# Column results of five experts turned by VectorE in 32x32 squares and scattered as quarter rows

## The chip, the cores and the metric

The kernel runs on one core of one Trainium2 chip. The metric is the device time of one execution in microseconds. The kernel before takes 846.96 us, the median of three runs (845.41 to 847.40). Five engines are named here as the profile names them: PE (TensorE, with PEld for its weight loads), DVE (VectorE), ACT (ScalarE), POOL (GpSimd) and SP (the queue that issues most DMAs).

## The reference, cut to what matters

Over 2048 tokens of 512 features the program returns `x + A(xn) + B(xn)`, where `xn` is the layer norm of `x`, A is a linear attention block and B a mixture of eight experts. Only B is touched here:

```python
logits = xf @ w_gate                       # 8 experts, each token takes its two best
gates = softmax(topk_val)
for e in range(E):                         # xf: (2048, 512), w1: (512, 1792), w2: (1792, 512)
    w = (gates * (topk_idx == e)).sum(-1, keepdims=True)
    out = out + w * (silu(xf @ w1[e]) @ w2[e])
```

## The kernel before, in words

The first quarter of the program (up to about 200 us) does the layer norm, the attention block and the routing. The rest goes through the experts in the order of how many tokens they have, numbered r = 0 to 7. Expert r has room for CAP[r] tokens: 576, 552, 544, 528, 520 for r = 0 to 4 and 512 for the others. The 1792 hidden features are taken in seven pairs j = 0 to 6 of 256; `g = 7 r + j` counts the pairs through.

**One pair.** `pair_fast` computes 256 hidden features in seven products (px, pz, py, L1129) with fp32r matmuls. Each operand is a high and a low part, which ACT and DVE make from a loaded weight (`split_hi` L126, `split_lo` L129). Between the products it calls `fill(k)`, which issues the waiting matmuls of the second layer (`mm2`) of the pair before, and `jobs(k)`, which issues the work that `plan` has put into slot k (0 to 6) of this pair. So the order on every engine's queue is written out by hand, and all engines take their instructions in that order.

**The second layer.** `mm2` adds up `h @ w2` in PSUM over all 14 hidden tiles. For the first 256 tokens of an expert with more than 512 places the result has the tokens on the partitions (L1058, "by token"). For the other 264 to 320 tokens the result is turned: the 512 output features stand on the partitions in four accumulators and the tokens in the columns (L1061, "by column"). The experts r = 5 to 7 (`single`) are by token altogether.

**Getting the results out.** By token: `put` multiplies by the token's gate on the way out of PSUM (DVE L1033 or ACT L1031) into a tile `yo`, and POOL adds `yo` to the rows of `out` in DRAM with an indirect accumulating DMA (L1035), after a small memset that it uses as a spacer (L1034). By column: ACT copies each accumulator into a tile `yt` (L1071); two pairs later `y_out` lets PE turn four 128x128 blocks of `yt` into a PSUM tile `yp` (L1093, a tile of the tag `mm`, which px, pz and py use too), and `put` on ACT, the memset and the scatter follow. There are three `y_out` for each of the five experts; `plan` puts two ahead of the first product of pair j = 2 of the next expert and one ahead of that of j = 3. Each scatter waits for the scatters of the expert before (`scat`).

**Weights.** SP loads w1 and w2 of each pair into one of three stage buffers as soon as one of them is free (`fetch_w`, L824 and L828). The w1 of a pair is used first by four DVE sums (`w1_sums`, L862 to L866), then by splits; w2 by splits only (`w2_hi`, `w2_lo`).

**The next expert's tokens.** POOL gathers them by indirect DMA (L921) in pair j = 3, two experts ahead; SP writes them to a DRAM scratch and reads them back (L975, L983); DVE turns them in 32x32 squares (`x_turn`, L992).

Of the kernel before, what the change touches and what calls it, by code (L numbers as in the profile page):

```python
# [72 lines left out]
def linear_attn_plus_moe(  # L73
# [132 lines left out]
    def constants_b():  # L206
        def iota(t, pattern, base=0, cm=0):
            G.iota(t, pattern=pattern, base=base, channel_multiplier=cm,
                   allow_small_or_imprecise_dtypes=True)

        G.memset(eps6, 1e-6)
        G.memset(ones, 1.0)
        G.affine_select(out=tri_b, in_=ones_b, pattern=[[1, P]], compare_op=ALU.is_ge,
                        fill=0.0, base=-1, channel_multiplier=-1)
        G.affine_select(out=bmask, in_=ones.rearrange("p (a b) -> p a b", a=8),
                        pattern=[[-DH, 8], [0, DH]], compare_op=ALU.is_ge,
                        fill=0.0, base=0, channel_multiplier=1)
# [162 lines left out]
    gate = rt.tile([P, OV0], F32, name="gate")  # L380
    eid_i = rt.tile([P, E], I32, name="eid_i")
    trip_i = rt.tile([P, 1], I32, name="trip_i")
    gidx = rt.tile([P, NB], I32, name="gidx")
    sidx = rt.tile([P, NB], I32, name="sidx")

# [206 lines left out]
    def table_end():  # L592
# [5 lines left out]
        V.scalar_tensor_tensor(sidx, t1, -1.0, em, op0=ALU.add, op1=ALU.add)  # L598
        Q.dma_start(gi_d, gidx[:, OV0:])
        Q.dma_start(si_d, sidx[:, OV0:])  # L600

    def side_jobs():
        yield from routing()
# [229 lines left out]
    def plain_w():  # L833
        if plain[0] > NPLAIN:
            return
        m, (r, j) = items[plain[0]]
        plain[0] += 1
        w = (W1, W2)[m][r, j] = hilo(sm, f"w{m}_{r}_{j}", (KC, 2)[m])
        split(w[0], w[1], wst.pop((m, r, j)))
        fetch_w()  # L840

    def w2_hi(r, j, i):
        if i == 0:
            W2[r, j] = hilo(sm, f"w2_{r}_{j}", 2)
        split_hi(W2[r, j][0][:, i, :], wst[1, r, j][:, i, :])

    def w2_lo(r, j, i):
        split_lo(W2[r, j][0][:, i, :], W2[r, j][1][:, i, :], wst[1, r, j][:, i, :])
        if i == 1:
            wst.pop((1, r, j))  # L850
            fetch_w()
# [175 lines left out]
    def put(r, i, src, w, eng):  # L1027
        b = r * RB + i
        yo = ta(f"yo{r}_{i}")
        if eng is A:  # L1030
            A.activation(yo[:w], src[:w], AF.Copy, scale=gate[:w, b:b + 1])  # L1031
        else:
            V.tensor_scalar(yo[:w], src[:w], gate[:w, b:b + 1], None, op0=ALU.mult)  # L1033
        G.memset(spacer, 0.0)  # L1034
        st = G.indirect_dma_start(out=out, out_offset=IOA(ap=sidx[:w, b:b + 1], axis=0),  # L1035
                                  in_=yo[:w], in_offset=None, compute_op=ALU.add).ins
        for s_ in scat[r]:
            tc.declare_no_dep(st, s_, reason="an expert's places hold different rows")
        for s_ in scat.get(r - 1, ()):
# [7 lines left out]
    def mm2(r, n, d):  # L1047
# [17 lines left out]
        if tok:  # L1065
            put(r, by_token(r)[d], ya[r, d], P, (V, A)[d % 2])
            return
        q = d - nt
        if q % 2 == 0:
            yt[r, q // 2] = raw(um(f"yt{r}_{q}"))[:, :2 * (N - nt * P)].rearrange("p (k c) -> p k c", k=2)  # L1070
        A.activation(yt[r, q // 2][:, q % 2, :], ya[r, d], AF.Copy)  # L1071

    def nacc(r):
        return 4 if single(r) else 2 + KC
# [21 lines left out]
    def pair_plain(r, j, fill, jobs, held):  # L1096
        n = half(r)
# [268 lines left out]
    def plan(g):  # L1366
# [44 lines left out]
                on(k, f, r + 1, name)  # L1411
        if r > 0 and j == 0:
            on(0, x_lo, r, "T4")
        if r > 0 and not single(r - 1):
# [134 lines left out]
```

## Time and profile before

| | value |
|---|---|
| median of three runs | 846.96 us (845.41 to 847.40) |
| the profiled execution | 845.64 us, of which the span of its instructions is 844.0 us |
| PE busy | 834.8 us (99%) |
| DVE, ACT, POOL busy | 80%, 64%, 21% of the span |
| granted clock of PE | 1.0 of full speed over the span |

The span runs from the first to the last instruction that the profile shows; 1.64 us of the profiled execution lie outside it. Busy shares are means over stages of different kinds, and a matmul's end is modelled, so PE's own rows say how often a matmul starts better than how long one lasts. An idle time is put down to what ended it.

### The profile page before, as it was taken

To read this page: it belongs to the slowest core of one execution; us is meant where nothing else is said; L and a number is where in the kernel's file an instruction comes from. 1 tells how busy PE (TensorE), PEld (TensorE's weight loads), DVE (VectorE), ACT (ScalarE), POOL (GpSimd) and SP (SyncE) were. 2 spreads that over 40 slices of the span, in tenths; PEclk is the share of its full clock that TensorE was granted. 3 is DMA by queue.
4 is the path that set the end of the run, shared out by engine and by line. 5 is a ranking of instruction groups with operands and counts; after the bars stand their busy time and mean duration, and the time that the engine had idled before them with its cause. 6 is when DMAs were issued, how large, how long until landed. Compare 5 with 4: busy or idle time off the path is not lost.

```text
span 844.0 us, 15824 instructions
## 1 busy us (share of the span) xinstructions
PE 834.8 (99%) x5454; PEld 764.2 (91%) x5454; DVE 676.0 (80%) x1495; ACT 539.0 (64%) x1127; POOL 178.6 (21%) x200
## 2 busy tenths in 40 slices
PE   8999999999999999999999999999999999999997
PEld 7899878788999999999999999999989999999986
DVE  7888888988878877888788778779888887987741
ACT  5566454348566766766777677667767766776740
POOL 2432224374410122014102300320130030020011
PEclk9999999999999999999999999999999999999999
DMA  5542036454755565566556744755665573349416
GB/s 178 165 159 75 26 107 216 132 178 162 219 165 140 155 138 162 134 158 161 154 136 166 178 122 138 166 153 147 160 167 145 146 189 100 100 118 265 131 15 163
DMA packets 94997, 124.23 MB, mean 147 GB/s; under 512 B 12354, under 2 KB 57794, under 8 KB 94882
## 3 DMA queue, kind: packets, MB, share of 16 engines
q1 hardware_dynamic: 86210, 103.18, 41.1%
q0 software_dynamic: 7840, 18.57, 11.1%
q10 hardware_dynamic: 864, 1.44, 0.5%
q8 instruction: 44, 0.72, 0.3%
q14 instruction: 39, 0.32, 0.1%
HBM read 93.56 MB, written 30.91 MB: 147 GB/s over the span
## 4 chain that ended last, share of the span: by engine, by line
PE 88%; DVE 7%; DMA 1%; ACT 1%; issue 1%; POOL 1%; SPq 0%; POOLq 0%; DVEq 0%
PE y L1058 25%; PE px L1129 19%; PE y L1061 13%; PE pz L1129 9%; PE k L325 5%; PE py L1129 5%; PE gacc L370 4%; PE op L1238 3%; PE qp L1187 2%; PE yp L1093 1%; DMA xg<-xn_d,gidx 1%; PE xtp L287 1%; DMA x<-in_A_x_dram 1%; PE hp L1108 1%; DVE den L1215 1%
## 5 line engine op out<-in xcount | busy, mean ns | idle before, releaser
L1035 POOL DMA_INDIRECT out_dram<-yo,sidx x37 | 61.2, 1654 | 486.4 <-DVE yo L1033 408.4
L129 DVE TENSOR_TENSOR h<-hs,h 128x512 fp32r<-128x512 f32 (+5 forms) x112 | 78.5, 701 | 6.9 <-ACT h L126 6.6
L126 ACT ACTIVATE h<-hs 128x512 fp32r<-128x512 f32 (+5 forms) x112 | 72.5, 647 | 2.9
L1137 ACT ACTIVATE hs<-px 128x256 f32<-128x256 f32 (+5 forms) x54 | 21.1, 391 | 57.8 <-PE px L1129 57.8
L1152 ACT ACTIVATE hs<-hs 128x256 f32<-128x256 f32 (+5 forms) x54 | 23.1, 427 | 46.9 <-DVE hs L1151 46.9
L1156 DVE TENSOR_TENSOR hs<-px,hs 128x256 f32<-128x256 f32 (+5 forms) x54 | 23.4, 434 | 33.9 <-PE px L1129 33.9
L1151 DVE TENSOR_TENSOR hs<-pz,hs 128x256 f32<-128x256 f32 (+5 forms) x54 | 23.3, 432 | 30.8 <-PE pz L1129 30.8
L370 PE MATMUL gacc<-pkhl,xnhl 128*128 128x512 f32 x192 | 47.8, 398 | 0.0
L921 POOL DMA_INDIRECT xg<-xn_d,gidx x37 | 42.3, 1143 | 25.8 <-issue 11.2
L1162 DVE TENSOR_TENSOR hs<-py,hs 128x256 f32<-128x256 f32 (+5 forms) x54 | 23.4, 433 | 24.2 <-PE py L1129 24.2
L370 PEld LDWEIGHTS gacc<-pkhl,xnhl 128*128 128x128 f32 x192 | 34.9, 188 | 6.9 <-DVE pkhl L129 0.2
L1157 ACT ACTIVATE hs<-hs 128x256 f32<-128x256 f32 (+5 forms) x54 | 22.9, 424 | 20.7 <-DVE hs L1156 19.4
L1058 PE MATMUL y<-w_0h,h 128*128 128x512 f32 x88 | 33.8, 403 | 0.0
L1058 PE MATMUL y<-w_1h,h 128*128 128x512 f32 x88 | 32.6, 398 | 0.0
L1058 PE MATMUL y<-w_2h,h 128*128 128x512 f32 x88 | 32.5, 396 | 0.0
L1058 PE MATMUL y<-w_3h,h 128*128 128x512 f32 x88 | 32.5, 395 | 0.0
L1147 ACT ACTIVATE hs<-px 128x256 f32<-128x256 f32 (+5 forms) x54 | 21.2, 392 | 17.6 <-PE px L1129 16.7
L1058 PE MATMUL y<-w_4h,h 128*128 128x512 f32 x88 | 32.0, 394 | 0.0
L1058 PE MATMUL y<-w_6h,h 128*128 128x512 f32 x88 | 31.7, 394 | 0.0
L1058 PE MATMUL y<-w_5h,h 128*128 128x512 f32 x88 | 31.6, 393 | 0.0
L1196 ACT ACTIVATE e_q<-qp 128x512 f32<-128x512 f32 x16 | 9.6, 600 | 33.0 <-PE qp L1187 18.3
L354 POOL TENSOR_TENSOR zacc<-zacc,pk 128x512 f32<-128x512 f32 x14 | 18.1, 1296 | 50.2 <-DVE L L347 50.2
(517 smaller groups left out, 3112.5 us busy)
## 6 DMA issues: line engine op xcount, KB each, us to landing
wst<-in_B_w_dram SPq DMA_DIRECT2D x63, 512.0 KB, 3.7
wst<-in_B_w_dram SPq DMA_DIRECT2D x196, 128.0 KB, 2.5
xs_d<-xg SPq DMA_DIRECT2D x117, 64.0 KB, 1.8
xq<-xs_d SPq DMA_DIRECT2D x28, 256.0 KB, 4.0
x<-in_A_x_dram SPq DMA_DIRECT2D x27, 256.0 KB, 3.3
xn_d<-xn SPq DMA_DIRECT2D x16, 256.0 KB, 2.5
out_dram<-x SPq DMA_DIRECT2D x11, 256.0 KB, 2.2
out_dram<-zt SPq DMA_DIRECT2D x5, 256.0 KB, 4.2
```

The lines of the kernel that those rows point to most:

```text
L126: A.activation(hi, src, AF.Copy)
L129: V.tensor_tensor(lo, src, raw(hi), op=ALU.subtract)
L325: T.matmul(o, xT(t, a, kc), w[b][:, kc, :], start=(j == 0), stop=(j == 11))
L370: T.matmul(gacc[d], xnhl[:, a, d * P:(d + 1) * P], pkhl[:, b, :], start=(t == 0 and i == 0), stop=(t == NT - 1 and i == 2))
L921: G.indirect_dma_start(out=t, out_offset=None, in_=xn_d, in_offset=IOA(ap=gidx[:, b:b + 1], axis=0))
L1035: st = G.indirect_dma_start(out=out, out_offset=IOA(ap=sidx[:w, b:b + 1], axis=0), in_=yo[:w], in_offset=None, compute_op=ALU.add).ins
L1058: T.matmul(ya[r, d], h[a][:, d * P:(d + 1) * P], w[b][:, n % 2, :], start=(first and i == 0), stop=(last and i == 2))
L1061: T.matmul(ya[r, d], w[a][:, n % 2, (d - nt) * P:(d - nt + 1) * P], h[b][:, nt * P:], start=(first and i == 0), stop=(last and i == 2))
L1129: T.matmul(ps_, w[a][:, o + kc, :], x[b][:, kc, :], start=(start and kc == 0 and i == 0), stop=(kc == 1 and i == 2), skip_group_check=True)
L1156: V.tensor_tensor(c22, px, c22, op=ALU.add)
L1162: V.tensor_tensor(c11, pz_, c11, op=ALU.add)
L1238: T.matmul(op, pqT[t][:, a, kc * P:(kc + 1) * P], M_v[kc // 2][b][:, kc % 2, :], start=(kc == 0 and i == 0), stop=(kc == KC - 1 and i == 2))
```

## The change

PE no longer turns the column results. `yt` is padded to a multiple of 32 tokens; POOL multiplies it by the gates (`y_gate`), which lie along the columns now and come as a row broadcast to all partitions through DRAM (`gate_out`, `gate_in`); DVE turns it in 32x32 squares into a tile `yu` (`y_turn`); POOL scatters it in groups of 32 tokens, where each partition holds a quarter of a token's row (`y_put`). For this the columns of w2 are written in another order when they are split (`columns`, `squares`), and results by token are put back in order on their way out of PSUM (`in_order`). `places` makes the row numbers of the quarter rows, once. `YMOVES` says in which pair, slot and for which expert each step is issued. The diff without the parts that only declare tiles or set constants (two DRAM scratch tensors, five POOL memsets, three views):

```diff
+YMOVES = {0: ((6, "i", -1),),
+          1: ((0, "g", -1, 0), (1, "g", -1, 1)),
+          2: ((0, "o", 0),),
+          3: ((3, "t", -1, 0, 0), (5, "t", -1, 0, 1)),
+          4: ((0, "p", -1, 0), (1, "t", -1, 1, 0), (2, "t", -1, 1, 1), (3, "t", -1, 2, 0), (4, "t", -1, 2, 1),
+              (5, "p", -1, 1), (6, "p", -1, 2))}
...
+    def columns(r, ap):
+        return ap if single(r) else ap.rearrange("p (a k i) -> p k a i", a=4, i=BLK)
+
+    def squares(r, ap):
+        return ap if single(r) else ap.rearrange("p (k a i) -> p k a i", a=4, i=BLK)
+
+    def in_order(r, ap):
+        return ap if single(r) else ap.rearrange("p (k a i) -> p a k i", a=4, i=BLK)
...
-        split_hi(W2[r, j][0][:, i, :], wst[1, r, j][:, i, :])
+        split_hi(squares(r, W2[r, j][0][:, i, :]), columns(r, wst[1, r, j][:, i, :]))
...
-        split_lo(W2[r, j][0][:, i, :], W2[r, j][1][:, i, :], wst[1, r, j][:, i, :])
+        hi, lo = (squares(r, W2[r, j][h][:, i, :]) for h in range(2))
+        split_lo(hi, lo, columns(r, wst[1, r, j][:, i, :]))
...
+        frm = in_order(r, src[:w])
+        to = yo[:w] if single(r) else yo[:w].rearrange("p (a k i) -> p a k i", a=4, i=BLK)
         if eng is A:
-            A.activation(yo[:w], src[:w], AF.Copy, scale=gate[:w, b:b + 1])
+            A.activation(to, frm, AF.Copy, scale=gate[:w, b:b + 1])
         else:
-            V.tensor_scalar(yo[:w], src[:w], gate[:w, b:b + 1], None, op0=ALU.mult)
+            V.tensor_scalar(to, frm, gate[:w, b:b + 1], None, op0=ALU.mult)
+        scatter(r, out, sidx[:w, b:b + 1], yo[:w])
+
+    def scatter(r, rows, idx, src):
         G.memset(spacer, 0.0)
-        st = G.indirect_dma_start(out=out, out_offset=IOA(ap=sidx[:w, b:b + 1], axis=0),
-                                  in_=yo[:w], in_offset=None, compute_op=ALU.add).ins
+        st = G.indirect_dma_start(out=rows, out_offset=IOA(ap=idx, axis=0), in_=src, in_offset=None,
+                                  compute_op=ALU.add).ins
...
+            if n < n_:
+                G.memset(yt[r, q // 2][:, :, n:], 0.0)
+        A.activation(yt[r, q // 2][:, q % 2, :n], ya[r, d], AF.Copy)
...
-    def y_out(r, k, tag="mm"):
+    def places(k):
+        if k == 0:
+            s_at = ta("s_at", BLK)
+            V.transpose(s_at, s_of)
+            Q.dma_start(sx_d, s_at)
+            ta_in.append(ta("s_in", P))
+            s_in = ta_in[0].rearrange("p (c j) -> p c j", j=BLK)
+            for a in range(4):
+                Q.dma_start(s_in[a * BLK:(a + 1) * BLK], sx_d.rearrange("(c b) j -> b c j", b=BLK))
+        else:
+            s_in = ta_in.pop().rearrange("p (c j) -> p c j", j=BLK)
+            s_up = ta("s_up", P).rearrange("p (c b) -> p c b", b=BLK)
+            V.transpose(s_up, s_in)
+            V.tensor_scalar(sidx4, s_up, 4.0, part, op0=ALU.mult, op1=ALU.add)
+
+    def gate_out(r):
+        if not single(r):
+            b = r * RB + 2
+            Q.dma_start(gate_d[r].rearrange("(b p) -> p b", p=P), gate[:, b:b + 3])
+
+    def gate_in(r):
+        if not single(r):
+            gb[r] = ta(f"gb{r}", 3 * P)
+            Q.dma_start(gb[r], gate_d[r:r + 1].broadcast_to([P, 3 * P]))
+
+    def y_gate(r, q):
+        if not single(r):
+            y = yt[r, q]
+            G.tensor_tensor(y, y, gb[r][:, :y.shape[2]].unsqueeze(1).broadcast_to(list(y.shape)), op=ALU.mult)
+
+    def y_turn(r, k, q):
         if single(r):
             return
         i, o, w = by_column(r)[k]
-        p = psm(tag, f"yp{r}_{k}")
-        for d in range(KC):
-            T.transpose(p[:w, d * P:(d + 1) * P], yt[r, d // 2][:, d % 2, o:o + w], ident)
-        put(r, i, p, w, A)
+        c = -(-w // BLK)
+        if q == 0:
+            yu[r, k] = ta(f"yu{r}_{k}")[:, :c * P].rearrange("p (c f) -> p c f", f=P)
+        V.transpose(yu[r, k][:, :, q * 2 * BLK:(q + 1) * 2 * BLK].rearrange("p c (k i) -> p c k i", i=BLK),
+                    yt[r, q][:, :, o:o + c * BLK].rearrange("p k (c j) -> p c k j", j=BLK))
+
+    def y_put(r, k):
+        if not single(r):
+            y = yu.pop((r, k))
+            for c in range(y.shape[1]):
+                scatter(r, out.rearrange("s (a f) -> (s a) f", a=4), sidx4[:, c, 3 * r + k:3 * r + k + 1], y[:, c])
...
-            for k in {2: (0, 1), 3: (2,)}.get(j, ()):
-                front.insert(k % 2, lambda k=k: y_out(r - 1, k))
+        for k, f, e, *a in YMOVES.get(j, ()):
+            if 0 <= r + e < E:
+                on(k, (gate_out, gate_in, y_gate, y_turn, y_put)["oigtp".index(f)], r + e, *a)
+        if g in (2, 4):
+            on(6, places, g // 2 - 1)
```

In `YMOVES` the key is the pair j, and in each entry stand the slot, the step (i `gate_in`, g `y_gate`, o `gate_out`, t `y_turn`, p `y_put`), the expert counted from the one in work, and the step's own arguments.

## Rows read from the trace of the kernel before

**Rows 1.** The page of the profiled execution: the first line is the span, the second the busy time of each engine with its share of the span and its instructions.

```profile
span 844.0 us, 15824 instructions
PE 834.8 (99%) x5454; PEld 764.2 (91%) x5454; DVE 676.0 (80%) x1495; ACT 539.0 (64%) x1127; POOL 178.6 (21%) x200
```

**Rows 2.** The chain of waits that ended last, summed by line (shares of the span).

```profile
by line: PE y L1058 25.3%; PE px L1129 18.8%; PE y L1061 13.2%; PE pz L1129 9.4%; PE k L325 4.9%; PE py L1129 4.7%; PE gacc L370 3.6%; PE op L1238 2.9%; PE qp L1187 2.0%; issue 0.8%; PE yp L1093 0.8%; DMA xg<-xn_d,gidx 0.7%; PE xtp L287 0.7
```

**Rows 3.** The instructions that write or read the tile `yp`, whole span. Behind the count: shortest, median and longest duration in ns, first and last start in us, shapes.

```profile
L1093 PEld LDWEIGHTS yp<-ident,yt x60: 84/139/146, 300.1 to 625.5; 128*128 128x128 f32 x40, 128*64 128x64 f32 x4, 128*40 128x40 f32 x4, 128*32 128x32 f32 x4
L1093 PE MATMUL yp<-ident,yt x60: 270/272/277, 300.3 to 625.6; 128*128 128x128 f32 x40, 128*64 128x128 f32 x4, 128*40 128x128 f32 x4, 128*32 128x128 f32 x4
L1031 ACT ACTIVATE yo<-yp,gate x15: 677/688/695, 301.0 to 625.9; 128x512 f32<-128x512 f32 x10, 64x512 f32<-64x512 f32 x1, 40x512 f32<-40x512 f32 x1, 32x512 f32<-32x512 f32 x1
```

**Rows 4.** The timeline of PE, first around the two `y_out` of expert 0 (start us, length us, then the instruction), then three matmuls of 512 columns elsewhere.

```profile
300.28 0.60 PE L1093 MATMUL yp<-ident,yt 128*128 128x128 f32 x4
300.64 0.48 PE L1058 MATMUL y<-w_0h,h 128*128 128x512 f32 x1
...
301.42 0.60 PE L1093 MATMUL yp<-ident,yt 128*128 128x128 f32 x4
301.77 0.48 PE L1058 MATMUL y<-w_0h,h 128*128 128x512 f32 x1
...
302.55 0.42 PE L1129 MATMUL px<-xB,wa_2h 128*128 128x276 f32 x2
...
319.10 0.39 PE L1058 MATMUL y<-w_2h,h 128*128 128x512 f32 x1
319.33 0.40 PE L1058 MATMUL y<-w_2l,h 128*128 128x512 f32 x1
319.56 0.63 PE L1058 MATMUL y<-w_2h,h 128*128 128x512 f32 x2
```

**Rows 5.** Busy time by stretch. A stretch goes from one pair's first copy out of px (L1137) to the next pair's. The columns are the stretch, its length, busy us and instructions of PE, PEld, DVE, ACT and POOL, the granted clock, the share of the DMA engines and GB/s. The first six stretches belong to expert 5 (pairs j = 0 to 5; the three `y_out` of expert 4 fall into the second and third), the last three to expert 6 (j = 0 to 2, without any `y_out`).

```profile
594.94:606.02 11.08, 11.08 (x84) 10.55 (x83) 9.61 (x20) 8.22 (x20) 0.13 (x1) 1.00 0.53 155
606.02:617.05 11.03, 11.03 (x73) 9.89 (x72) 9.05 (x24) 8.00 (x18) 5.21 (x6) 1.00 0.80 183
617.05:628.05 11.00, 11.00 (x72) 9.80 (x71) 9.10 (x22) 7.33 (x17) 2.84 (x5) 1.00 0.66 143
628.05:638.59 10.54, 10.54 (x68) 9.51 (x67) 8.29 (x18) 6.75 (x15) 4.62 (x6) 1.00 0.73 203
638.59:649.12 10.53, 10.53 (x68) 9.51 (x67) 7.42 (x16) 7.65 (x17) 0.00 (x0) 1.00 0.37 102
649.12:659.66 10.54, 10.54 (x68) 9.53 (x67) 9.57 (x20) 7.65 (x18) 0.00 (x0) 1.00 0.57 149
670.19:681.12 10.93, 10.93 (x71) 9.91 (x70) 9.45 (x20) 7.93 (x18) 1.22 (x1) 1.00 0.47 145
681.12:691.26 10.14, 10.14 (x65) 9.12 (x64) 8.98 (x24) 6.75 (x17) 5.47 (x8) 1.00 0.99 226
691.26:701.79 10.53, 10.53 (x68) 9.52 (x67) 8.87 (x22) 6.75 (x15) 0.00 (x0) 1.00 0.48 135
```

**Rows 6.** Groups of DVE instructions by line, tile and shape: count, busy us and mean ns of one, then idle time before them.

```profile
L992 DVE STREAM_TRANSPOSE xr<-xq 128x256 f32<-128x256 f32 x56 | 21.4, 420 | 0.0
L129 DVE TENSOR_TENSOR pkhl<-pk,pkhl 128x512 fp32r<-128x512 f32 x16 | 14.2, 889 | 0.8 <-ACT pkhl L126 0.7
L129 DVE TENSOR_TENSOR w_6l<-wst,w_6h 128x512 fp32r<-128x512 f32 x16 | 10.9, 683 | 0.0
L129 DVE TENSOR_TENSOR wa_3l<-wst,wa_3h 128x512 fp32r<-128x512 f32 x8 | 5.5, 681 | 0.0
```

**Rows 7.** The same of POOL's instructions.

```profile
L1035 POOL DMA_INDIRECT out_dram<-yo,sidx x37 | 61.2, 1654 | 486.4 <-DVE yo L1033 408.4 <-ACT yo L1031 73.7 <-issue 1.3
L1034 POOL MEMSET spacer<- 1x1 f32 x37 | 19.3, 521 | 7.2 <-issue 7.2
L354 POOL TENSOR_TENSOR zacc<-zacc,pk 128x512 f32<-128x512 f32 x14 | 18.1, 1296 | 50.2 <-DVE L L347 50.2
```

**Rows 8.** The timeline of POOL at two scatters that follow each other.

```profile
291.28 1.64 POOL L1035 DMA_INDIRECT out_dram<-yo,sidx  x1 [55.29 <-DVE yo L1033]
292.35 0.61 POOL L1034 MEMSET spacer<- 1x1 f32 x1
293.22 1.57 POOL L1035 DMA_INDIRECT out_dram<-yo,sidx  x1 [0.26 <-issue]
```

**Rows 9.** DMA queues of the page (packets, MB, share of 16 engines' span): q1 carries what SP issues, q0 POOL's gathers and scatters.

```profile
q1 hardware_dynamic: 86210, 103.18, 41.1%
q0 software_dynamic: 7840, 18.57, 11.1%
```

**Rows 10.** The timeline of SP in pairs j = 4 and 5 of expert 5: loads of w1 (four issues) and w2, and eight writes of 64 KB in rows of 512 bytes. The last row is the issues of the four-part loads of w1, with the median us from issue to landing at its end.

```profile
637.87 1.87 SPq L824 DMA_DIRECT2D wst<-in_B_w_dram  x4
644.32 0.39 SPq L828 DMA_DIRECT2D wst<-in_B_w_dram  x1
...
650.64 3.75 SPq L975 DMA_DIRECT2D xs_d<-xg  x8
...
wst<-in_B_w_dram SPq DMA_DIRECT2D x196, 128.0 KB, 2.5
```

**Rows 11.** The timeline of DVE in the same pairs: the first use of the w1 that was issued at 637.87.

```profile
645.88 0.42 DVE L862 TENSOR_TENSOR wr<-wst 128x256 f32<-128x256 f32 x1
```

More of the change, by code (lines that the diff above doesn't have):

```diff
@@ L35 @@
 CAP = (576, 552, 544, 528, 520, 512, 512, 512)
+NCOL = sum(c > 4 * 128 for c in CAP)
 UW = 2 * CAP[0]
@@ L99, in linear_attn_plus_moe @@
     xs_d = tc.dram_tile((E * RB * P, D), F32, name="xs_d")
+    gate_d = tc.dram_tile((E, 3 * P), F32, name="gate_d")
+    sx_d = tc.dram_tile((P, BLK), F32, name="sx_d")
     def ta(name, w=D, dt=F32):
@@ L231, in constants_b @@
             G.memset(i_cap[:, r:r + 1], float(CAP[r]))
+        G.memset(gate, 0.0)
+        for a in range(4):
+            G.memset(part[a * BLK:(a + 1) * BLK], float(a))
         G.affine_select(out=lower, in_=ones[:, :E * E].rearrange("p (a b) -> p a b", a=E),
@@ L382, in linear_attn_plus_moe @@
     trip_i = rt.tile([P, 1], I32, name="trip_i")
+    s_of = i_e8.rearrange("p t e -> p (t e)")[:, :BLK]
+    part = rt.tile([P, 1], F32, name="part")
+    sidx4 = L.rearrange("p t e -> p (t e)").bitcast(I32).rearrange("p (c b) -> p c b", b=BLK)
     gidx = rt.tile([P, NB], I32, name="gidx")
@@ L600, in table_end @@
         Q.dma_start(si_d, sidx[:, OV0:])
+        t3, e3 = (a[:, :NCOL * RB].rearrange("p (r i) -> p r i", i=RB)[:, :, 2:] for a in (t1, em))
+        V.scalar_tensor_tensor(s_of[:, :3 * NCOL].rearrange("p (r i) -> p r i", i=3), t3, -1.0, e3,
+                               op0=ALU.add, op1=ALU.add)
     def side_jobs():
@@ L838, in plain_w @@
         w = (W1, W2)[m][r, j] = hilo(sm, f"w{m}_{r}_{j}", (KC, 2)[m])
-        split(w[0], w[1], wst.pop((m, r, j)))
-        fetch_w()
+        st = wst.pop((m, r, j))
+        if m:
+            for i in range(2):
+                split(squares(r, w[0][:, i, :]), squares(r, w[1][:, i, :]), columns(r, st[:, i, :]))
+        else:
+            split(w[0], w[1], st)
+        fetch_w()
+    def columns(r, ap):
[4 more added lines that the diff above has]
+        return ap if single(r) else ap.rearrange("p (k a i) -> p a k i", a=4, i=BLK)
     def w2_hi(r, j, i):
@@ L1067, in mm2 @@
             return
-        q = d - nt
+        q, n = d - nt, N - nt * P
+        n_ = -(-n // BLK) * BLK
         if q % 2 == 0:
-            yt[r, q // 2] = raw(um(f"yt{r}_{q}"))[:, :2 * (N - nt * P)].rearrange("p (k c) -> p k c", k=2)
-        A.activation(yt[r, q // 2][:, q % 2, :], ya[r, d], AF.Copy)
+            yt[r, q // 2] = raw(um(f"yt{r}_{q}"))[:, :2 * n_].rearrange("p (k c) -> p k c", k=2)
+            if n < n_:
+                G.memset(yt[r, q // 2][:, :, n:], 0.0)
+        A.activation(yt[r, q // 2][:, q % 2, :n], ya[r, d], AF.Copy)
     def nacc(r):
@@ L1085, in pieces @@
         return [lambda c=c, d=d: mm2(r, c, d) for c, d in order]
-    def y_out(r, k, tag="mm"):
+    gb, yu = {}, {}
+    ta_in = []
+    def places(k):
[5 more added lines that the diff above has]
+            s_in = ta_in[0].rearrange("p (c j) -> p c j", j=BLK)
+            for a in range(4):
+                Q.dma_start(s_in[a * BLK:(a + 1) * BLK], sx_d.rearrange("(c b) j -> b c j", b=BLK))
+        else:
+            s_in = ta_in.pop().rearrange("p (c j) -> p c j", j=BLK)
[15 more added lines that the diff above has]
+    def y_turn(r, k, q):
         if single(r):
@@ L1413, in plan @@
             on(0, x_lo, r, "T4")
-        if r > 0 and not single(r - 1):
-            for k in {2: (0, 1), 3: (2,)}.get(j, ()):
-                front.insert(k % 2, lambda k=k: y_out(r - 1, k))
+        for k, f, e, *a in YMOVES.get(j, ()):
[3 more added lines that the diff above has]
+            on(6, places, g // 2 - 1)
         if j == 3 and r in (E // 2, E - 1):
```

## The prediction

> **What bounds the kernel now.** I read the page first: PE is busy 99% of a span of 844.0 us, DVE 80%, ACT 64% and POOL 21% [rows 1]. A busy PE need not be the limit, since ends of matmuls are modelled, so the chain of waits came next: 71% of it is PE's second layer and products (L1058, L1061, L1129), most of the rest PE's earlier matmuls, and the turning of the column results (L1093) has 0.8% [rows 2]; 0.8% of 844 is 6.75 us. The decisive view is the busy time by stretch. In expert 6, where nothing is turned, a pair takes 10.53 us, and so does a pair of expert 5 with DVE 7.42 us busy and one with DVE 9.57 us busy (10.54 us) [rows 5]. The pair does not get longer when DVE has 2 us more to do, so PE's stream of matmuls sets its length, and DVE can fill 91% of a pair without showing. What is taken off PE in these stages should come off the time, until another engine or a load is late.
>
> **What the change removes.** Sixty PE transposes in fifteen `y_out`, and fifteen evictions on ACT of 688 ns [rows 3]. A transpose's own 272 ns is no price, because matmuls overlap; I count from start to start. From 300.28 to 302.55 PE starts two `y_out` of four transposes and six matmuls of 512 columns: 2.27 us. Such a matmul otherwise starts every 0.23 us (319.10, 319.33, 319.56), six take 1.38, and (2.27 - 1.38) / 2 = 0.44 us is left for one `y_out` [rows 4]. A second reading: the two stretches of expert 5 that hold the three `y_out` of expert 4 last 11.03 + 11.00 = 22.03 us, the same two of expert 6 10.14 + 10.53 = 20.67; the difference of 1.36 us is 0.45 for each [rows 5]. All have a moving side of 128 columns, the short last blocks too [rows 3], so fifteen cost 6.6 us (0.44) to 6.8 us (0.45). All of it is on PE's chain. I take 6.6. ACT's 10.3 us hide nothing, ACT has a third of each stretch free [rows 5]. The buffer of the tag `mm` that `yp` took comes free for px and pz; since PE shows no idle time in those stretches, I count nothing for it.
>
> **What it adds.**
>
> *DVE.* Per expert four transposes of 256 columns and two of 64 or 128. `x_turn` makes the same kind with the same 32-wide runs: 420 ns for 256 columns [rows 6]. With at most 0.28 us for a short one (estimate, between half of it and a little more) that is 4 x 0.42 + 2 x 0.28 = 2.2 us per expert, 0.84 in pair j = 3 and 1.4 in j = 4. There DVE is busy 8.29 of 10.54 and 7.42 of 10.53 us [rows 5], and gets 9.1 and 8.8, less than the 9.57 that costs nothing in j = 5. Price: 0. Without that cover it would be at most 11 us for the five experts.
>
> *The order of w2's columns.* Splits on ACT and DVE read 32-wide runs instead of 512 in one piece; by-token evictions likewise. The number of elements stays. A split whose source is strided (128-wide runs) takes 681 ns, one in a piece 683 [rows 6]. So I take 0, and can't see a gain. No row has a split with 32-wide runs; were it twice as long, DVE would get 2 x 0.68 us more in a pair j = 5 with 0.97 us free [rows 5], and the loss were 0.4 us in each of the ten fullest pairs, 4 us: the upper bound. One w2 split of pair 0 becomes two halves, 2 x 0.68 us on DVE, once: 0 (within 0.3).
>
> *POOL.* Ten `y_gate` of 528 to 640 columns. The sum into `zacc` takes 1296 ns for 512 [rows 7], so 1.3 to 1.6 us each, 15 us in all. Scatters: groups of 32 tokens make 4 + 4 + (2, 2, 1, 1, 1) for the five experts, 47 in the place of 15. One follows another after 1.94 us, memset and all [rows 8]; a train of ten takes 19.4 us, from j = 4 to the end of j = 5, where POOL is idle (0.00 busy) [rows 5]. In order behind the train stand only the next expert's pads and token scatters, more than a pair later, and the gathers of j = 3 come ahead of it. Price: 0. The fronts of the train wait for DVE's `y_turn`, and only their own train waits behind them. `y_gate` waits for the gates' DMA; behind it on POOL are the gathers, two pairs later.
>
> *The port between POOL and DVE.* A split beside POOL's sums into `zacc` (`pkhl`) takes 889 ns on average, 683 elsewhere [rows 6], 0.2 us more. Two `y_gate` in j = 1 put 0.4 us on DVE's 9.05 of 11.03 us [rows 5]: hidden. At worst a DVE instruction waits out the whole of a 1.3 us `y_gate`; two of these are 2.6 us against 1.98 free, 0.6 us per expert, 3 us in all.
>
> The Trainium skill, GPSIMD Engine Reference, section 1 (Specifications), says that POOL's way to SBUF is shared with VectorE and contended by DVE instructions with two SBUF inputs, which the splits are. By that rule every split beside `y_gate` loses time and the sum goes towards the 3 us; the 889 ns above agree that there is such a loss, and show it as 0.2 us.
>
> *SP.* `gate_out` and `gate_in` are ten small DMAs, each issued pairs ahead of its use. `places` stops SP once, in pair 2 of expert 0: its read-back waits for its write to land, and the next weight load stands behind. A w1 load issued from 637.87 to 639.74 lands 2.5 us later, about 642.2, and is first used at 645.88 [rows 10, 11]: 3.7 us to spare. Price 0, at most 2 us once.
>
> **Sum.** -6.6 us on PE, all else hidden: 845.64 - 6.6 = 839.0 us for the profiled execution. The median of the runs shown is 1.3 us above that execution, 846.96, so the forecast is **840.4 us**.
>
> **Rivals.**
>
> *The gain is eaten by DVE.* The upper bounds above come together: 4 us from split order, 3 from the port, and the time is 846.96 - 6.6 + 7 = 847.4, no change; half of it gives 843.9. For it: DVE is the second busiest engine, and 9.57 of 10.54 us leaves little. Against it: the stretch with 9.57 us is no longer than that with 7.42, and none of the new transposes falls in j = 5 or 6.
>
> *The quarter rows clog the DMA engines and weights come late (slower).* 1440 whole-row packets (ten blocks of 128 tokens and 160 tokens in the short ones) become 47 x 128 = 6016 of 512 bytes, 1200 per expert within the train's 19.4 us. A packet of q0 takes 0.111 x 16 x 844 / 7840 = 0.19 us on average [rows 9]. If an accumulating packet costs this whatever its size, a train needs 1200 x 0.19 / 16 = 14.3 us of all sixteen engines. With the other traffic at 0.57, the share of j = 5 [rows 5], 8.3 us are free; loads come 6.0 us late, 3.7 are spare, and PE loses 2.3 us per expert, 11.5 in all: 846.96 - 6.6 + 11.5 = 851.9 us. It turns the sign when the loss passes 1.3 us per expert, at (8.3 + 3.7 + 1.3) x 16 / 1200 = 0.18 us per packet. Against it: packets of q1, 1.2 KB on average, take 0.411 x 16 x 844 / 86210 = 0.064 us [rows 9], and SP sends eight writes of 128 rows of 512 bytes in 3.75 us [rows 10], which is 0.06 us per packet if the engines keep up. Twice that, for a read and a write, is 0.12 and stays below the point. Also, a stretch with the engines at 0.99 of their time kept its 10.14 us [rows 5].
>
> The Trainium skill, DMA: Bandwidth & Descriptors, section Bandwidth, speaks for this rival: transfers under 64 KB are dominated by their descriptors, and here whole-row scatters of 256 KB are cut to 64 KB. By that rule the packets would not get cheaper as they get shorter and the time is the 851.9 above; q1's packets speak against it, and no row has a short accumulating one.
>
> **How the numbers follow.** Forecast 0.68 (own range 839.5 to 842); part or all of the gain eaten by DVE 0.19, of which 0.07 still gains over 0.3%; DMA late 0.13, mostly slower. A measurement of this kernel tells 0.3%, 2.5 us, from no change. So faster 0.74, same 0.13, slower 0.13. The range goes from 838.6 (6.8 us of gain, and 1.55 us by which the lowest of the three runs lies under their median) to 846.0, which takes in most of the second case; the third is left out.
>
> **What would show it.** Right: no L1093; the second and third stretch of experts 1 to 5 shorter by 0.89 and 0.46 us and all other stretches as before; transposes of 0.42 us into `yu`; w2 splits at 0.68; trains of scatters at 1.9 us and POOL at about 0.9 in j = 4 and 5; PE without idle time. Wrong in its first step: L1093 gone and the stretches as long as before. DVE's case: PE waits for DVE at px or pz in j = 1 or 5, splits of w2 above 0.8 us. DMA's case: packets of q0 near 0.19 us still, and DVE or ACT waiting for `wst` in j = 5 and 6. The forecast is wrong if the median is above 844.4.

## The result, and the profile after

The changed kernel takes **852.43 us** (median of 20 runs, 847.61 to 858.84) against 846.95 us (20 runs, 845.31 to 850.21): 1.0071 times as long, with an interval of 1.0058 to 1.0085. The forecast was 840.4 us, the range ended at 846.0, and the change is slower by 5.5 us. The profiled execution is a long one of 856.27 us, with a span of 854.5.

These lines of its page stand beside [rows 1, 2, 7, 9]: span, busy times, queues, the chain by line, and the group of the quarter-row scatters.

```profile
span 854.5 us, 15872 instructions
PE 833.5 (98%) x5394; PEld 761.6 (89%) x5394; DVE 692.5 (81%) x1530; ACT 529.9 (62%) x1113; POOL 251.4 (29%) x285
...
q1 hardware_dynamic: 89650, 104.25, 43.6%
q0 software_dynamic: 12896, 18.71, 13.2%
...
PE y L1096 23%; PE px L1210 17%; PE y L1099 11%; PE pz L1210 9%; PE k L337 5%; PE py L1210 4%; PE gacc L382 4%; DMA wst<-in_B_w_dram 3%; PE op L1319 3%; PE qp L1268 2%; DVE h L138 1%; DVE w_1l L138 1%; DMA xg<-xn_d,gidx 1%; PE xtp L299 1%; DMA x<-in_A_x_dram 1%
...
L1073 POOL DMA_INDIRECT out_dram<-yu,L x47 | 78.7, 1675 | 99.3 <-DVE yu L1168 88.4
```

PE's 60 transposes are gone (5454 to 5394 matmuls) and yet the span is 10.5 us longer, with 21 us instead of 9 in which PE does nothing. The weight load `wst` has 3% of the chain, some 25 us; it is not among the lines of [rows 2].

Busy time by stretch, cut and with columns as in [rows 5]. The first four are pairs j = 1 to 4 of expert 2, the fifth is j = 4 of expert 4, the last two are j = 1 and 2 of expert 5.

```profile
373.37:384.17 10.80, 10.80 (x76) 10.15 (x75) 9.06 (x21) 6.96 (x16) 8.33 (x7) 1.00 0.82 206
384.17:395.63 11.46, 11.46 (x79) 10.71 (x78) 7.09 (x19) 7.06 (x15) 3.40 (x5) 1.00 0.98 170
395.63:413.67 18.04, 13.41 (x80) 12.79 (x80) 12.23 (x28) 7.16 (x15) 1.59 (x2) 0.81 0.36 83
413.67:424.86 11.19, 11.19 (x80) 10.68 (x79) 9.30 (x23) 7.96 (x18) 9.58 (x13) 1.00 0.71 129
569.55:584.60 15.05, 12.26 (x79) 11.72 (x80) 11.70 (x27) 7.91 (x18) 11.00 (x14) 0.89 0.55 106
617.05:627.18 10.13, 10.13 (x65) 9.11 (x64) 8.77 (x20) 6.75 (x17) 7.33 (x6) 1.00 0.89 213
627.18:637.71 10.53, 10.53 (x68) 9.51 (x67) 8.53 (x22) 6.53 (x15) 3.27 (x4) 1.00 0.81 203
```

The last two are the stretches that held `y_out`: 20.66 us where they were 11.03 + 11.00 [rows 5], so the gain on PE is there. But one pair took 18.04 us and another 15.05 where the same pairs take 11.18 and 10.69 when nothing is late (in gate_rows below). In the first, PE stands idle for 18.04 - 13.41 = 4.63 us, and its busy time is 13.41 - 11.18 = 2.23 us more than the same 80 matmuls take there, at a granted clock of 0.81.

What the pair of 18.04 us waits for, from three views: SP's timeline (start, length), the chain in order of time, and busy time in slices of 2 us (columns as in [rows 5]).

```profile
384.94 2.10 SPq L842 DMA_DIRECT2D wst<-in_B_w_dram  x4
387.08 0.44 SPq L1149 DMA_DIRECT2D gate_d<-gate  x1
...
391.23 0.39 SPq L846 DMA_DIRECT2D wst<-in_B_w_dram  x1
```

```profile
386.75 11.25 DMA wst<-in_B_w_dram
...
398.13 0.44 DVE wr L895
...
399.70 0.62 DVE h L138
...
400.36 0.85 PE y L1099 x2
```

```profile
394.00:396.00 2.00, 1.73 (x11) 1.37 (x9) 0.00 (x0) 0.56 (x2) 0.00 (x0) 1.00 0.35 34
396.00:398.00 2.00, 0.00 (x0) 0.00 (x0) 0.00 (x0) 0.03 (x1) 0.00 (x0) 0.98 0.54 58
398.00:400.00 2.00, 0.00 (x0) 0.00 (x0) 1.84 (x5) 0.63 (x1) 0.00 (x0) 0.50 0.56 115
400.00:402.00 2.00, 1.64 (x7) 1.65 (x8) 2.00 (x5) 0.00 (x0) 0.00 (x0) 0.50 0.14 49
402.00:404.00 2.00, 2.00 (x10) 2.00 (x10) 1.27 (x3) 0.92 (x2) 0.00 (x0) 0.50 0.38 109
404.00:406.00 2.00, 2.00 (x16) 2.00 (x14) 0.92 (x3) 0.82 (x2) 0.00 (x0) 0.82 0.55 152
```

The last part of a w1 load, issued at 386.75, lands after 11.25 us instead of 2.5 [rows 10]. DVE waits for it with its first sum (L895), the split of `h` for the second layer stands behind that sum in DVE's order, and PE waits for `h`. While PE is idle its clock falls to 0.50, which is the level of 1.2 GHz; it starts again at 400.36, gets 10 matmuls of the usual 16 or so into 2 us, and has its full clock back between 404 and 406. So the late load costs 4.63 us of idle time and 2.23 us of slow matmuls.

Right behind the w1 load SP issues `gate_out` (L1149): three columns of `gate`, 384 values of four bytes each, written next to each other in DRAM. In the same stretch of time the DMA engines look like this (slice, granted clock, DMA share, GB/s; a packet counts with its whole time in the slice in which it begins, so a share can pass 1):

```profile
388.00:390.00 2.00, 1.00 0.98 273
390.00:392.00 2.00, 1.00 0.95 237
392.00:394.00 2.00, 1.00 2.06 35
```

The packets that begin between 392 and 394 take over twice all sixteen engines' time in sum, while 35 GB/s get through, and 34 in the next 2 us. The scatters of quarter rows are not there yet, so they are not the cause. What is there is a gather (POOL's timeline):

```profile
381.73 1.29 POOL L954 DMA_INDIRECT xg<-xn_d,gidx  x1
...
387.67 1.14 POOL L954 DMA_INDIRECT xg<-xn_d,gidx  x1 [0.72 <-issue]
...
412.08 1.82 POOL L1073 DMA_INDIRECT out_dram<-yu,L  x1 [23.18 <-DVE yu L1168]
414.21 1.80 POOL L1073 DMA_INDIRECT out_dram<-yu,L  x1 [0.26 <-issue]
```

The gathers are put into pair j = 3 by the plan, but they run in j = 1 and 2 of this expert: in POOL's queue nothing stands ahead of them any more that waits for late data, as `y_out`'s scatters did. In the kernel before, the first of the same gathers comes some 15 us later, behind such a scatter (POOL's timeline there):

```profile
394.94 1.66 POOL L1035 DMA_INDIRECT out_dram<-yo,sidx  x1 [8.43 <-ACT yo L1031]
396.91 1.04 POOL L921 DMA_INDIRECT xg<-xn_d,gidx  x1 [0.30 <-DVE h L129]
```

So there were three theories. **G**: `gate_out`'s short neighbouring writes hold up the DMA engines. **T**: the early gathers collide with the w1 loads. **P**: the port between POOL and DVE, where `y_gate` stretches DVE's instructions; it would explain the smaller losses of 0.3 to 1.6 us in the pairs j = 2 of experts 1 to 4. The prediction's DMA rival, that quarter rows clog the engines, is a fourth, and every run that keeps the quarter rows and is fast speaks against it. In the texts put down before the runs G is theory A (A1 and A2 are two readings of it), T is rival B, the quarter rows are rival C, and P is theory D.

### The profile page after: what moved, and what is told of

It reads as the page before. It is cut to its first block, busy times and chain, and to the rows that moved or that the text cites. A ratio compares the mean times of both kernels' runs of the same rounds, so it can differ in the third digit from the quotient of the medians.

```text
span 854.5 us, 15872 instructions
## 1 busy us (share of the span) xinstructions
PE 833.5 (98%) x5394; PEld 761.6 (89%) x5394; DVE 692.5 (81%) x1530; ACT 529.9 (62%) x1113; POOL 251.4 (29%) x285
## 3 DMA queue, kind: packets, MB, share of 16 engines
q0 software_dynamic: 12896, 18.71, 13.2%
## 4 chain that ended last, share of the span: by engine, by line
PE 78%; DVE 11%; DMA 5%; ACT 1%; issue 1%; SPq 1%; POOL 1%; DVEq 0%; POOLq 0%
PE y L1096 23%; PE px L1210 17%; PE y L1099 11%; PE pz L1210 9%; PE k L337 5%; PE py L1210 4%; PE gacc L382 4%; DMA wst<-in_B_w_dram 3%; PE op L1319 3%; PE qp L1268 2%; DVE h L138 1%; DVE w_1l L138 1%; DMA xg<-xn_d,gidx 1%; PE xtp L299 1%; DMA x<-in_A_x_dram 1%
## 5 line engine op out<-in xcount | busy, mean ns | idle before, releaser
L1073 POOL DMA_INDIRECT out_dram<-yo,sidx x22 | 34.9, 1588 | 275.2 <-DVE yo L1068 270.8
L1073 POOL DMA_INDIRECT out_dram<-yu,L x47 | 78.7, 1675 | 99.3 <-DVE yu L1168 88.4
L1072 POOL MEMSET spacer<- 1x1 f32 x69 | 37.1, 538 | 7.5 <-issue 7.5
L895 DVE TENSOR_TENSOR wr<-wst 128x256 f32<-128x256 f32 x54 | 25.1, 465 | 14.5 <-DMA wst<-in_B_w_dram 14.5
L1096 PE MATMUL y<-w_0h,h 128*128 128x512 f32 x88 | 32.0, 393 | 0.0
```

Source lines behind the costliest of these rows:

```text
L895: V.tensor_tensor(s1, a21, a22, op=ALU.add)
L1073: st = G.indirect_dma_start(out=rows, out_offset=IOA(ap=idx, axis=0), in_=src, in_offset=None, compute_op=ALU.add).ins
L1096: T.matmul(ya[r, d], h[a][:, d * P:(d + 1) * P], w[b][:, n % 2, :], start=(first and i == 0), stop=(last and i == 2))
```

## The experiments

All twelve kernels were timed in rounds of runs against the kernel before, whose medians were 846.05 to 846.50 us. In the rounds of the changed kernel that median was 846.95, so a difference between two kernels of different rounds is uncertain by about a microsecond. The edits are shown without the lines that only declare a tile, and without one POOL memset of `gate` at the start, which the versions of the kernel before need.

| kernel | median us | ratio to before, interval |
|---|---|---|
| no_gate_out | 842.81 | 0.9960 (0.9947 to 0.9973) |
| before_gate_out | 852.09 | 1.0072 (1.0052 to 1.0093) |
| gathers_held | 844.80 | 0.9986 (0.9977 to 0.9994) |
| gate_rows | 844.49 | 0.9976 (0.9968 to 0.9985) |
| gate_rows_held | 843.87 | 0.9961 (0.9946 to 0.9975) |
| gates_on_dve | 871.66 | 1.0294 (1.0277 to 1.0310) |
| no_y_gate | 839.59 | 0.9916 (0.9901 to 0.9931) |
| before_gate_spread | 846.42 | 0.9998 (0.9988 to 1.0008) |
| before_gate_64 | 845.65 | 0.9996 (0.9987 to 1.0006) |
| before_gate_one | 849.46 | 1.0036 (1.0023 to 1.0050) |
| gates_late_dve | 839.52 | 0.9919 (0.9905 to 0.9933) |
| gates_late_pool | 844.19 | 0.9977 (0.9968 to 0.9986) |

**Take `gate_out` away, and put it alone into the kernel before.**

```diff
     def gate_out(r):
         if not single(r):
-            b = r * RB + 2
-            Q.dma_start(gate_d[r].rearrange("(b p) -> p b", p=P), gate[:, b:b + 3])
+            return
...
-            Q.dma_start(gb[r], gate_d[r:r + 1].broadcast_to([P, 3 * P]))
+            Q.dma_start(gb[r], x[r:r + 1, :3 * P].broadcast_to([P, 3 * P]))
```

> The changed kernel without gate_out: no gate is written to DRAM, and gate_in broadcasts a row of x in its place, so the results by column of five experts are scaled by other numbers; every other instruction and DMA stays. Theory A (the 384 four-byte writes of each gate_out hold the DMA engines up for 6 to 10 us, and the weight loads behind them come late): the stalls in pairs j = 2 to 4 vanish and the time is 846.95 - 6.6 = 840.4 us (839 to 842). Rival B (POOL's gathers, no longer queued behind the old scatters, run some 15 us earlier and collide with the weight loads): the gathers are as early as in the changed kernel, so the time stays at about 852 us. Rival C (the accumulating quarter rows clog the engines): also about 852 us.

842.81 us, 9.6 less than the changed kernel, although the quarter-row scatters and the early gathers are still there. It is 0.8 us above the range set for G; what is left falls into the pairs j = 2 (below).

```diff
+    def gate_out(r):
+        if not single(r):
+            b = r * RB + 2
+            Q.dma_start(gate_d[r].rearrange("(b p) -> p b", p=P), gate[:, b:b + 3])
...
+        if j == 2:
+            on(0, gate_out, r)
```

> The kernel before plus the five gate_out alone, in slot 0 of pair j = 2 as in the change, into a DRAM scratch that nobody reads. PE still turns the column results. Theory A: the DMA engines stall after each gate_out, weights come late and the time rises by about 12 us, to 853 to 860 us. Rivals B and C: nothing that they blame is in this kernel, so the time stays at 847 us (within 1 us).

852.09 us, just under the range: five small DMAs that nobody reads cost the kernel before 6.0 us. In its trace SP issues one at 468.38, right behind a w1 load, and in busy time by slices PE runs dry:

```profile
466.45 1.89 SPq L826 DMA_DIRECT2D wst<-in_B_w_dram  x4
468.38 0.47 SPq L1101 DMA_DIRECT2D gate_d<-gate  x1
```

```profile
476.00:478.00 2.00, 2.00 (x13) 1.67 (x13) 0.00 (x0) 1.48 (x3) 0.34 (x1) 1.00 0.75 66
478.00:480.00 2.00, 0.91 (x8) 0.70 (x6) 1.09 (x3) 0.59 (x2) 1.70 (x2) 1.00 0.95 94
```

DVE has nothing to do from 476 to 478 and PE is idle for half of the next 2 us. In all, DVE waits for weights like this (us, times, longest):

```profile
DVE wr L864 <- DMA wst<-in_B_w_dram: 10.2, 4, 3.4
```

Both runs speak for G. As this kernel has its gathers where they always were, T is not needed for a loss.

**Hold the gathers back.** The first gather of an expert waits for a DVE instruction of its own pair.

```diff
+        if i == 0 and r > 1:
+            V.memset(tick, 0.0)
+            G.tensor_tensor(spacer, tick, tick, op=ALU.add)
```

> The changed kernel with POOL's gathers for experts 2 to 7 held until DVE reaches slot 2 of pair j = 3, about where they ran before; gate_out stays. Rival B: the collisions are gone and the time is 840 to 842 us. Theory A: the stalls stay with gate_out, 849 to 855 us, perhaps a little less than the changed kernel since fewer transfers wait behind them. Rival C: 852 us.

844.80 us, 7.6 less than the changed kernel, between what B and A had said. The stall of the engines is still there (busy time by slices, SP having issued the w1 load at 385.74 and `gate_out` at 387.68), but PE does not notice:

```profile
390.00:392.00 2.00, 2.00 (x16) 1.91 (x16) 1.18 (x5) 1.19 (x4) 0.00 (x0) 1.00 0.00 0
392.00:394.00 2.00, 2.00 (x18) 2.00 (x17) 1.60 (x5) 1.78 (x5) 0.00 (x0) 1.00 1.89 16
394.00:396.00 2.00, 2.00 (x13) 1.73 (x13) 2.00 (x5) 0.96 (x2) 0.00 (x0) 1.00 0.34 31
```

The engines move 16 GB/s at a share of 1.89, yet PE is busy throughout, and DVE's first sum of this w1 runs at 393.33 without a wait. With no gather beside it the w1 load is through in time. So T is half right: here the early gathers decide whether the load falls into the stall. They are not the only way into it, since before_gate_out loses without them, and in gathers_held too the pair j = 3 of expert 0 takes 14.18 us where gate_rows has 11.87.

**Write the gates as rows**, twelve rows of 128 bytes in four DMAs, after DVE has turned them.

```diff
-            Q.dma_start(gate_d[r].rearrange("(b p) -> p b", p=P), gate[:, b:b + 3])
+            V.tensor_copy(g_col[:, :3], gate[:, b:b + 3])
+            V.transpose(g_row, g_col)
+            for c in range(4):
+                Q.dma_start(gate_d[r].rearrange("(b p) -> b p", p=P)[:, c * BLK:(c + 1) * BLK],
+                            g_row[c * BLK:c * BLK + 3, :])
```

> The changed kernel with gate_out made of rows: DVE turns the gates in 32x32 squares first and four small DMAs write 12 rows of 128 bytes in place of 384 single values. Same results as the reference. Theory A: the stalls vanish, 840 to 842 us, with three short DVE instructions and three more DMA issues per expert hidden. Rivals B and C: about 852 us.

844.49 us: the same gates by the same way, 7.9 us less than the changed kernel, but 2.5 us above the range set for G. The long pairs are gone (the stretch of 18.04 us is 11.18 again); pairs j = 2 still lose. With both edits:

> Both edits at once: gate_out as 12 rows of 128 bytes, and the gathers held to slot 2 of pair j = 3. If the short writes are the cause and the early gathers only decide how much of the stall reaches the weight loads (A with B), nothing is left to gain over either edit alone but the last 1 to 2 us: 842 to 843.5 us, that is 6.6 us of PE gained and some 3 us lost to y_gate. If each were a cause of its own (their losses add), the time would fall by 7 us more than with one edit, to 838 us or less.

843.87 us, 0.4 us above the range and hardly less than either alone. The two edits don't add up, because they remove the same loss: without the stall there is nothing for the gathers to worsen.

**How must the writes lie?** The kernel before with `gate_out` alone, its values 512 bytes apart, 64 bytes apart, and one packed column in the place of three:

```diff
-    gate_d = tc.dram_tile((E, 3 * P), F32, name="gate_d")
+    gate_d = tc.dram_tile((E, 3 * P, P), F32, name="gate_d")
...
-            Q.dma_start(gate_d[r].rearrange("(b p) -> p b", p=P), gate[:, b:b + 3])
+            Q.dma_start(gate_d[r, :, 0].rearrange("(b p) -> p b", p=P), gate[:, b:b + 3])
```

> The kernel before with the five gate_out alone, but each of the 384 values of four bytes goes 512 bytes from the next in DRAM. If short writes to neighbouring addresses are what stalls (A1): no stall, 846 to 847.5 us. If any write of four bytes stalls (A2): as with the packed gate_out, 851 to 853 us.

846.42 us, no loss. The 64-byte kernel has 16 in the place of `P`:

> The kernel before with gate_out alone, the 384 values 64 bytes apart in DRAM (512 bytes apart cost nothing, packed cost 6 us). If the stall needs several writes within one block of 64 bytes: 846 to 847.5 us; if it needs a wider neighbourhood: between that and 852 us.

845.65 us, no loss either. Both have as many four-byte writes as before_gate_out, issued at the same place behind the w1 load, so neither the number of descriptors nor their length is the price: it is that neighbouring writes fall closer than 64 bytes. The issues of `gate_d` land so, packed and then 64 bytes apart (the tile's view, which has a landing for three of the five packed issues and two of the others):

```profile
DMA to landing us min/median/max: 10.4/12.4/12.4
```

```profile
DMA to landing us min/median/max: 5.5/6.7/7.8
```

```diff
-            Q.dma_start(gate_d[r].rearrange("(b p) -> p b", p=P), gate[:, b:b + 3])
+            Q.dma_start(gate_d[r].rearrange("(b p) -> p b", p=P)[:, :1], gate[:, b:b + 1])
```

> The kernel before with gate_out alone, packed, but only one of its three columns: 128 writes of four bytes. If the stall grows with the number of writes that fall on the same addresses' neighbourhood: a third of the stall, which the 3.7 us of slack of the weight loads hide, 846 to 848 us; if it is one fixed stall per DMA: 851 to 853 us.

849.46 us: 3.3 us for a third of the packed writes, against 6.0 us for all. That lies between what the two theories had said: the loss grows with their number. Whether it does so in proportion the intervals don't tell (a third of 0.52 to 0.93% against 0.23 to 0.50%).

The Trainium skill, DMA: Bandwidth & Descriptors, section Specifications, says that transfers under 512 bytes are made by reading and writing back. By that rule all three spacings should pay alike; the runs show a loss only for the packed one. The Trainium skill, on the same page, section Rules for kernel authors, asks for a contiguous last dimension because each element becomes a descriptor of its own; gate_rows follows that rule and agrees, while before_gate_64 breaks it and costs nothing.

**What does gating on POOL cost?** On gate_rows_held, first without it:

```diff
     def gate_in(r):
...
+            return
     def y_gate(r, q):
         if not single(r):
-            y = yt[r, q]
-            G.tensor_tensor(y, y, gb[r][:, :y.shape[2]].unsqueeze(1).broadcast_to(list(y.shape)), op=ALU.mult)
+            return
```

> The same with no y_gate and no gate_in at all: the results by column of five experts are added without their gates. This gives the price of the gating by column. Theory D: 839.5 to 841 us, as with the gates on DVE. If the loss in pair j = 2 comes from the transposes into yu or from the scatters: 842 to 843.5 us, as gate_rows_held.

839.59 us, 843.87 - 839.59 = 4.3 us less. This is the whole price of ten `y_gate` and five `gate_in`, and what is left is the forecast's time within 0.8 us. Then the same instruction on DVE, in the same slots:

```diff
-            G.tensor_tensor(y, y, gb[r][:, :y.shape[2]].unsqueeze(1).broadcast_to(list(y.shape)), op=ALU.mult)
+            V.tensor_tensor(y, y, gb[r][:, :y.shape[2]].unsqueeze(1).broadcast_to(list(y.shape)), op=ALU.mult)
```

> The same with y_gate on DVE in place of POOL, same slots. Theory D (what is left in pair j = 2 of experts 1 to 4 is DVE, whose instructions with two SBUF inputs wait out POOL's y_gate): DVE gets two instructions of 0.8 us and loses no more than that, the stretches of j = 2 go back to the length of the others and the time is 839.5 to 841 us. If D is wrong: no change against gate_rows_held, or slower, since DVE then has 1.6 us more to do in a pair with 2 us free.

871.66 us, a miss by 30 us. The waits name it (us, times, longest):

```profile
DVE yt L1168 <- DMA gb<-gate_d: 30.9, 5, 7.2
```

`gate_in` is planned for the last slot of pair j = 0 and `y_gate` for the first of j = 1, so the gates have no pair in which to land. On POOL a late `gb` held up nobody but POOL; DVE takes its instructions in order, everything behind `y_gate` waits, and PE with it. The long pairs are now j = 1, 16 to 18 us each. The pairs j = 2 were free of loss, so P stood, but the slot was wrong. Hence one pair later, on gate_rows, with the product on DVE as above:

```diff
-          1: ((0, "g", -1, 0), (1, "g", -1, 1)),
-          2: ((0, "o", 0),),
+          2: ((0, "o", 0), (3, "g", -1, 0), (5, "g", -1, 1)),
```

> The changed kernel with gate_out as rows (gathers not held) and y_gate on DVE a pair later, in slots 3 and 5 of j = 2, when the gates have long landed. If theory D holds and the 872 us of the gates on DVE came from DVE waiting in order for the gates' DMA: both waits are gone, no stretch is longer than its pair, 839.5 to 841 us. If DVE simply has no room for 1.5 us more: pairs j = 2 stay long by about a microsecond each and the time is 843 us or more.

**839.52 us**, 0.81% faster than the kernel before (0.67 to 0.95%) and level with no_y_gate, but with the whole computation. The first two lines of its page:

```profile
span 837.5 us, 15886 instructions
PE 828.4 (99%) x5394; PEld 758.0 (91%) x5394; DVE 691.8 (83%) x1550; ACT 530.2 (63%) x1113; POOL 236.6 (28%) x275
```

The same slots, with the product left on POOL:

> The same with y_gate left on POOL, in slots 3 and 5 of j = 2. If DVE's instructions wait out POOL's wherever it runs: 842 to 844 us, with the loss moved to a stretch later; if only the sums of w1 at the end of j = 1 were sensitive: 840 to 841.5 us.

844.19 us. The later slot gives POOL nothing (gate_rows has 844.49): it sets the order in POOL's queue, and POOL goes ahead as soon as the operands are there (four of its five waits end with the landing of `gb`), in this trace a pair before the slot's own. So the loss did not move to a later stretch, as the text before the run had it. These two kernels differ only in the engine of `y_gate`, so the 844.19 - 839.52 = 4.7 us between them are P's. First DVE beside POOL's `y_gate` at 297.94, and POOL's own row with the second of its two products once more by itself (gates_late_pool), then the stretch that follows in it, and the same pair in gates_late_dve:

```profile
298.33 1.73 DVE L137 TENSOR_TENSOR w_1l<-wst,w_1h 128x512 fp32r<-128x512 f32 x1
299.98 1.78 DVE L895 TENSOR_TENSOR wr<-wst 128x256 f32<-128x256 f32 x1
301.80 0.42 DVE L896 TENSOR_TENSOR wr<-wr,wst 128x256 f32<-128x256 f32 x1
...
297.94 3.54 POOL L1163 TENSOR_TENSOR yt<-yt,gb 128x640 f32<-128x640 f32 x2 [3.66 <-PE py L1214]
299.48 2.00 POOL L1163 TENSOR_TENSOR yt<-yt,gb 128x640 f32<-128x640 f32 x1
...
302.13:315.16 13.03, 11.68 (x80) 11.04 (x80) 11.56 (x31) 7.13 (x15) 5.18 (x6) 1.00 0.71 190
```

```profile
302.02:313.45 11.43, 11.43 (x80) 10.88 (x79) 10.20 (x26) 7.12 (x15) 2.58 (x4) 1.00 0.71 197
...
307.25 0.80 DVE L1163 TENSOR_TENSOR yt<-yt,gb 128x640 f32<-128x640 f32 x1
```

A DVE sum of 0.42 us takes 1.78 and a split of 0.68 takes 1.73 while POOL makes its two products. Each begins 0.4 to 0.5 us into one of them and ends 0.3 to 0.6 us behind its end (at about 299.5 and at 301.48). The two together put DVE 1.73 + 1.78 - 0.68 - 0.42 = 2.4 us behind, and the pair that follows is 13.03 - 11.43 = 1.6 us longer. The other pairs j = 2 are 11.85, 12.00 and 11.58 us against 11.18, 10.91 and 10.69, so the four lose 4.2 us of the 4.7. On DVE the same product takes 0.80 us and hides in DVE's free time.

## Why the prediction was wrong

The forecast counted one gain and put every price at 0. The gain came; two of the prices were not 0 and outweighed it.

**PE's gain of 6.6 us: right.** Expert 5's two stretches lost 22.03 - 20.66 = 1.37 us for three `y_out` (forecast 0.89 + 0.46), and all of it shows where nothing new is late: gates_late_dve is 6.6 us under the kernel before of its own runs, 846.14 - 839.52, and its span 6.5 us under the 844.0 of [rows 1].

**DVE's transposes and the order of w2: right at price 0.** `y_turn` takes 0.44 us, the splits of w2 are still 0.68 as in [rows 6], and PE shows no idle time in the stretch that holds most of the transposes (413.67 to 424.86, DVE 9.30 us busy).

**POOL's trains of scatters, and the DMA rival.** Right at price 0, with 1675 ns of POOL for each scatter of quarter rows where one of whole rows had 1654 [rows 7], and 9.58 and 11.00 us of POOL in pairs j = 4. The rival's price was 851.9 us, and that the measured time is close is luck, for its cause is not the one: the long waits come ahead of a train, and of the versions with the trains and without packed writes all are under the kernel before, but for gates_on_dve, whose wait is another. A packet of q0 takes 0.132 x 16 x 854.5 / 12896 = 0.14 us on average over gathers, whole and quarter rows, under the 0.18 at which that rival would have turned the sign. The Trainium skill, DMA: Bandwidth & Descriptors, section Bandwidth, calls transfers under 64 KB descriptor-dominated. The quarter-row scatters stand at that edge with 64 KB each, and no run here shows a loss from them.

**The step that failed is "SP": "`gate_out` and `gate_in` are ten small DMAs, each issued pairs ahead of its use", price 0.** The working asked only when the data of these DMAs are needed, and which load stands behind them on SP. It did not ask what a DMA of 384 four-byte pieces does to transfers already under way on the same engines. That is the largest term: 852.43 - 844.49 = 7.9 us by gate_rows, 852.43 - 842.81 = 9.6 by no_gate_out, or 0.9 us less in both if each kernel is set against the kernel before of its own rounds. Part of it is PE at half its clock, 2.23 us in the pair of 18.04. The 3.7 us that a w1 load has to spare were read rightly [rows 10, 11]; it came 8.75 us late. "Pairs ahead" holds for `gate_out` only: `gate_in` is issued one slot ahead of `y_gate`, in the changed kernel at 373.57 for a product that begins at 378.29, once `gb` has landed. On POOL this cost nothing that shows; on DVE it is the 30.9 us of waits in gates_on_dve.

**"The port between POOL and DVE": the mechanism right, the size wrong.** It was priced at 0, with 3 us at worst and 0.2 us for each split from `pkhl` [rows 6]. Measured, it is 1.0 to 1.4 us for each DVE instruction that meets a `y_gate`, and in all 3.4 us (842.81 - 846.05 + 6.6, in no_gate_out), 4.3 us (no_y_gate) or 4.7 us (gates_late_pool against gates_late_dve): more than the worst case. The 889 ns are an average over sixteen splits, which are far from alike (the tile `pkhl` in the trace before; shortest, median and longest in ns):

```profile
L129 DVE TENSOR_TENSOR pkhl<-pk,pkhl x16: 656/672/1776, 16.4 to 105.6; 128x512 fp32r<-128x512 f32 x16
```

Five of them begin within the first 0.7 us of a sum into `zacc` and take 1.23 to 1.78 us; the eleven others, which meet none or only its last 0.1 us, take 0.66 to 0.77. So the price of a meeting stood in the trace before, and the average over all sixteen was taken for it; the bound from the other side, that a DVE instruction waits out one on POOL, was near the true value. The Trainium skill, SBUF — State Buffer, section SBUF: two separate sides, states that the port pair is held for a whole instruction and the other engine blocks. The trace agrees: the sum that begins 0.5 us into the second `y_gate`, of 2.00 us, ends 0.28 us behind it.

**POOL's order: missed.** The prediction left the gathers "two pairs later" behind `y_gate`. In a queue that is only an order: with `y_out`'s scatters gone from in front of them they ran some 15 us earlier, beside w1 loads. That alone costs at most about 1 us (gate_rows against gate_rows_held), but it puts the loads into the stall: 852.43 against 844.80 with the gathers held.

The sum from the runs: 846.95 - 6.6 on PE + 4.3 for gating on POOL (no_y_gate) + 7.9 for packed writes (gate_rows) = 852.6, against a measured 852.43. The last term is taken from the changed kernel itself, so what this tests is the rest: 846.05 - 6.6 + 4.3 = 843.75 against the 844.49 of gate_rows in the same rounds. In the profiled execution the pairs add up too: 6.86 and 4.36 us in the two shown, 1.88 in pair 3 of expert 0, 0.43 in pair 3 of expert 4 and 3.3 in the pairs j = 2, less 6.6, make 10.2 of the 10.5 us between the spans.

What stays open: why packed short writes hold all the engines up (the traces show that they do, not where the writes queue), which spacing under 64 bytes is enough, and why the loss of the changed kernel varies so much from run to run (847.61 to 858.84).

## What to carry to other kernels

A small DMA is priced by how its bytes lie at the destination and by what is in flight beside it, not by its size or by when its result is needed: write a column of scalars as rows, or at least 64 bytes apart, and look for the load that was issued just before it. When a step leaves a queue, ask what then runs earlier on that engine, since a slot in a plan is an order and not a time. An elementwise product for an idle POOL is not free when DVE has two-input work at that time; on DVE it can be cheaper, if its operand has surely landed.

## What was not expected of the hardware

Five DMAs of 1.5 KB each cost 6.0 us in a kernel of 846 (852.09 against 846.05), and nothing when the same values lie 64 bytes apart (845.65 against 846.14). During such a stall the sixteen engines moved 16 and 35 GB/s, with records that sum to 1.89 and 2.06 of their time. And 4.63 us without work on PE were followed by some 4.4 us at 1.2 GHz, which added 2.23 us to the loss.
